# A Mamba-2 scan and ReGLU kernel: pairs 4 and 5 turned by DMA, block 0's tail in another order, its stores issued by GpSimd

## The chip, the core and the metric

The kernel runs on one core of a Trainium2 chip. A core has five engines, each with an instruction queue of its own that it works through in order: TensorE (PE in the profile, its weight loads PEld), VectorE (DVE), ScalarE (ACT), GpSimd (POOL) and SyncE (SP), which here does nothing but issue DMA transfers. They meet through semaphores. The metric is the device time of one execution in microseconds (us); the kernel before takes 122.76 us, the median of three runs from 122.37 to 123.28.

## The reference

Four batches of eight heads with 768 steps each go through a state-space scan in chunks. Its output, 3072 tokens by 256 features, goes through a gated feed-forward layer. Cut to what matters:

```python
for c in range(nc):                                  # chunks of the sequence
    cum = np.cumsum(log_a[:, :, sl], axis=-1)
    L = np.exp(cum[:, :, :, None] - cum[:, :, None, :]) * causal
    y[:, :, sl] = ((Cc @ Bc.T) * L) @ xc             # inside the chunk
                + (Cc @ state) * np.exp(cum)         # from the chunks before
    state = np.exp(sum(la)) * state + (Bc * decay_from_j).T @ xc
gate = np.maximum(X @ w_gate, 0.0)                   # X: [3072, 256], w: [256, 1536]
out  = (gate * (X @ w_val)) @ w_out                  # w_out: [1536, 256]
```

`B` and `C` have 16 features a head, `x` has 32.

## The kernel before

The kernel uses chunks of 128 steps, two chunks of one batch to a **pair**: there are twelve pairs, three to a batch, and six feed-forward **blocks** of 512 tokens, two pairs each. The decays are not put into the matrix L; they are multiplied into `B` and `C` beforehand (`fac`), so that L becomes a mere causal mask.

A pair goes through these steps. Its raw `B` and `C` (`bcr`) and `x` (`xr`) are loaded by SyncE. They are scaled to bf16 by `scale_bc`, `scale_one` or `scale_padded`; `x` is cast to `xb` by `to_x`. `B` and `C` have to be **turned**, features to the partitions. Up to pair 5 TensorE does that (`transp`, line 389, called by `turn`); `tevac` copies the result out of PSUM, `B` in one copy (`bevac`, BT) and `C` in two (`cevac`, CT), each with half of the heads masked to zero. From pair 6 on (`NDMA = 6`) GpSimd writes the scaled `B` and `C` into a zero-padded tile `bz` (`turned`, three in rotation), and one DMA transpose, issued by SyncE on line 306, gives the turned tile `TT`. For the first four pairs, which are laid out "wide", the turned `B` is also turned back (`back`, `backevac`, tile `bx`).

Then `G` (line 452), or `G_rows` (line 491) from pair 6 on, makes the products of `C` and `B`, four PSUM banks a pair. `gevac` brings them to `gs` under the causal mask: ScalarE copies one and a half banks, which GpSimd masks in place (`causal`, line 171), and VectorE masks the others while it copies (lines 475 and 479). `Dm` (line 630), the visit of D, multiplies `gs` with `x`; `inter` (line 619) adds the part of the state, both into the tile `y`; `yevac` copies `y` to `yT`, the feed-forward's input. `state`, `states` (line 569) and `states_two` (line 693) add the products of `B` and `x` into the state's bank `A_ps`, `spread` and `sums_two` take the running sum to the form that `inter` wants. From block 2 on two pairs are taken together (`Dm_two`, line 678).

A block's feed-forward is, for each of its twelve slices of 128 of the 1536 features, `gv` (gate and val on 512 tokens, line 738) or two `gvh` (256 tokens each, line 753): ScalarE applies the relu (`r`), VectorE multiplies (`h`). `fout` (line 783) multiplies `h` with `w_out`, and `foevac` copies the result `o` to `ob` and stores it.

The order is written out by hand. `in_order` ties every engine to the order of the program's text, so a wait of one instruction holds all that stand behind it on its engine. Block b works on its own feed-forward and, between its matmuls, on pairs P = 2b+2 and Q = 2b+3, which block b+1 needs; W = 2b+1 is the pair that the block before left to be finished. The shared PSUM banks are five (`bank`), and the tags "tp", "y" and "Aps" have one bank each.

SyncE's queue is a list too: loads, DMA transposes and stores are issued in the text's order. GpSimd's list holds the masks, the scaling of later pairs and the casts of their `x`; the loop of block 2 calls `scale(Q + 2)`, that is pair 9, just before the masks of pairs 6 and 7.

Of the kernel before, what the change touches and what calls it, by code (L numbers as in the profile page):

```python
# [8 lines left out]
FP32 = mybir.dt.float32  # L9
# [20 lines left out]
def kernel(  # L30
# [71 lines left out]
    def load(p, q):  # L102
        if "bcr" not in st.setdefault(p, {}):
            new_bc(p)
        load_bc(p, 1, q)
        load_bc(p, 0, q)
        new_x(p)
        for i in range(2):
            load_x(p, i, q)
# [182 lines left out]
    def scale_padded(p, eng):  # L292

        b, c0, _ = place(p)
        z = turned[p % 3]
        f = fac[:, b, c0:c0 + 2].rearrange("s i j h -> s i (j h)")
        eng.tensor_tensor(  # L297
            out=z.rearrange("s (i k) (h n) -> s i (k h) n", k=4, n=N)[:, :, 0:2 * NH],
            in0=st[p]["bcr"].rearrange("s i j h n -> s i (j h) n"),
            in1=f.to_broadcast([128, 2, 2 * NH, N]), op=ALU.mult)  # L300
        parts = z.rearrange("s (i k) (q t n) -> s i k t q n", k=4, q=4, t=2)
        for t in range(2):
            eng.tensor_copy(out=parts[:, :, 2 + t, t], in_=parts[:, :, 1, t])
        st[p]["B"] = [z[:, 4 * i] for i in range(2)]
        tt = st[p]["TT"] = att.tile([128, 8, 128], BF16, tag="TT", name="TT", bufs=4)
        nc.sync.dma_start_transpose(out=tt, in_=z.rearrange("s k n -> s (k n)"))

    def new_bs(p):
        st[p]["bs"] = att.tile([128, 4, 128], BF16, tag="bs", name="bs", bufs=6)
# [59 lines left out]
    def scale(p, eng):  # L369
        if p >= NDMA:  # L370
            scale_padded(p, eng)
        else:
            new_bs(p)
            scale_bc(p, eng)
        to_x(p, eng)
# [41 lines left out]
    def ct(p, i, rows=slice(0, 128), t=None):  # L417
        if p < NWIDE:
            c = st[p]["CT"][rows, :, :, 64 * i:64 * i + 64]
        else:  # L420
            c = st[p]["CT"][rows, :, i]
        return c if t is None else c[:, t]

    def split(p, ap):

        return ap.rearrange("s t (r m) -> s t r m", r=2) if p < NWIDE else ap
# [17 lines left out]
    def G(p):  # L444
        s = st[p]
        if "gp" not in s:
            G_banks(p)
        g = s["gp"]
        for i in range(2):
            for q in range(4):  # L450
                r = slice(32 * q, 32 * q + 32)
                nc.tensor.matmul(  # L452
                    out=split(p, g[q][:, i]), lhsT=s["BT"][r, i], rhs=ct(p, i, r),
                    start=(i == 0), stop=True, tile_position=(32 * q, 0),
                    skip_group_check=True)
        s["gs"] = att.tile([128, 4, 4, 128], BF16, tag="gs", name="gs", bufs=2)
# [70 lines left out]
    def state(p, i):  # L527
        astep(p, i)
        sevac(p, i)
# [93 lines left out]
    def Dm(p, apart=False):  # L623
        s = st[p]
        y_bank(s, apart)
        for t in range(2):
            for i in range(2):
                new = opening(s, t)
                for q in range(4):
# [4 lines left out]
                        start=new, stop=True,  # L634
                        tile_position=(0, 32 * q), skip_group_check=True)

    def yevac(p, *engs):
        s = st.pop(p)
        dst = yT[:, :, p * 256:(p + 1) * 256]
        if p >= NWIDE:  # L640
            copy(engs[0], dst.rearrange("q t (i m) -> q t i m", i=2), s["ya"])
            return
        for t in range(2):
            copy(engs[t % len(engs)],
                 dst[:, t].rearrange("q (i m r) -> q i r m", i=2, r=2),
                 s["y"][t].rearrange("q i (r m) -> q i r m", r=2))
# [154 lines left out]
    def foevac(b, ts, o=None):  # L801
        last = b == NBLK - 1 and ts == 2
        if ts % 2 == 0 and not last:
            return
        ob = ffn.tile([128, 2, DM], FP32, tag="ob", name="ob", bufs=3)
        r0 = b * 512 + ts * 128
        if last:
            nc.scalar.copy(out=ob[:, 0], in_=fst["o"][:, 0])
            nc.scalar.dma_start(out=out[r0:r0 + 128, :], in_=ob[:, 0])
            return  # L810
        nc.scalar.copy(out=ob, in_=o or fst["o"])  # L811
        rows = out[r0 - 128:r0 + 128, :].rearrange("(i p) m -> p i m", p=128)
        for part in ((slice(0, 1), slice(1, 2)) if b in (2, 3) and ts == 3 else (slice(0, 2),)):
            nc.sync.dma_start(out=rows[:, part], in_=ob[:, part])


    B_, C_ = slice(0, 1), slice(1, 2)
# [89 lines left out]
    def turn(p):  # L907
        transp(p, 1)
        transp(p, 0)

    def tevac(p, beng, *cengs):
        bevac(p, beng)
        cevac(p, *cengs)
# [49 lines left out]
    for b in range(NBLK):  # L963
        P, Q, W = 2 * b + 2, 2 * b + 3, 2 * b + 1
        more = P < NPAIR
        if b == 1:
            load(P + 2, nc.sync)
            load(P + 3, nc.sync)
        if b == 2:
            scale(Q, nc.gpsimd)  # L970
            load(Q + 2, nc.sync)

        nh = (4, 6, 8, 0)[min(b, 3)]
        for f in range(nh):
            if b == 0:
                continue
            turning = f == (3 if b == 1 else nh - 3)
            gvh_mm(b, f, 0)
            gvh_relu(b, f, 0)
            gvh_mul(b, f, 0)  # L980
            if b == 1 and f == 1:
                to_x(P, nc.scalar)
            if turning:
                inter(W, 0)
                inter(W, 1)
                Dm(W)
                if b == 1:
                    states(P)
                    scale_one(P, nc.gpsimd, 1)
                else:  # L990
                    states_two((P, Q))
                yevac(W, nc.scalar)
                if b == 1:
                    spread(P)
                else:
                    sums_two((P, Q))
# [4 lines left out]
        for f in range(nh, NF):  # L1001
            gv(b, f, b > 2 and f == 0)
            if b == 0:
                if f == 5:
                    over_sum(de_ps)
                if f == 7:
                    sevac(1, 1)
                if f == 9:
                    turn(P)
                    tevac(P, nc.scalar, nc.vector)  # L1010
                if f == 10:
                    held(Q, bc=False)
                if f == 11:
                    back(P)
                    backevac(P, nc.scalar)
            elif b == 1:
                if f == nh:
                    turn(P)
                    tevac(P, nc.scalar, nc.vector)
                    scale(Q, nc.gpsimd)  # L1020
                if f == 8:
                    turn(Q)
                    tevac(Q, nc.scalar, nc.vector)
                    scale(Q + 1, nc.gpsimd)
                    load(Q + 3, nc.sync)
            elif b == 2:
                if f == 9:
                    scale(Q + 2, nc.gpsimd)
                    load(Q + 3, nc.sync)
                    load(Q + 4, nc.sync)  # L1030
            elif b == 3:
                if f in (2, 6):
                    scale(P + 2 + f // 4, nc.gpsimd)
# [3 lines left out]
        if b == 0:  # L1037

            for third in range(3):
                fs = range(4 * third, 4 * third + 4)  # L1040
                fout(b, 0, fs)
                fout(b, 1, fs)
                if third == 0:
                    new_bc(Q + 1)
                    nc.vector.memset(st[Q + 1]["bcr"][0:1, 0, 0, 0, 0:1], 0.0)
                    load_bc(Q + 1, 0, nc.sync)
                    new_x(Q + 1)
                    for i in range(2):
                        load_x(Q + 1, i, nc.sync)
                    load_bc(Q + 1, 1, nc.sync)  # L1050
                    for n in range(1, NB):
                        nc.vector.reciprocal(fac[:, n, :, 0], fac[:, n, :, 1])
                if third == 0:
                    turn(Q)
                if third == 1:
                    G(P)
                    gevac(P)
                    tevac(Q, nc.scalar, nc.vector)
            foevac(b, 1)
            to_x(Q, nc.scalar)  # L1060
            fout(b, 2)
            state(P, 0)
            state(P, 1)
            held(Q + 2)
            back(Q)
            backevac(Q, nc.vector)
            fout(b, 3, range(6))
            inter(P, 0)
            inter(P, 1)
        elif b == 1:  # L1070
            fout(b, 0)
            G(P)
# [36 lines left out]
            continue  # L1109
        Dm(P)  # L1110
        states(Q)
        if b == 0:
            yevac(P, nc.vector)
            G(Q)
            gevac(Q, after={3: lambda: spread(Q)})
            new_bs(Q + 1)
            scale_one(Q + 1, nc.gpsimd, 0)
        else:
            yevac(P, nc.scalar)
            G(Q)  # L1120
            spread(Q)
            gevac(Q)
        fout(b, 3, range(6, NF) if b == 0 else range(NF))
        foevac(b, 3)

    in_order(tc)
# [30 lines left out]
```

## Time and profile before

| | |
|---|---|
| three runs | 122.37, 122.76, 123.28 us |
| profiled execution | 122.67 us |
| its span, first to last instruction | 121.0 us |
| granted TensorE clock | 1.00 |
| busy: PE, DVE, ACT, POOL | 115.5, 89.0, 74.3, 51.5 us |
| packets of SyncE's loads, transposes and stores | 73088, 10.54 MB |
| DMA transposes | 6, 256 KB of bf16 each |

A line of a timeline gives the start in us from the span's beginning, the length, the engine, the kernel's line, the operation, the tile written and the tile read, and how many instructions are merged; in square brackets stands how long the engine had been idle and what ended that. "SPq" marks the issue of a DMA on SyncE; the length of such a line is that of the issue, not of the transfer. The chain of work that ended last is followed back from the last instruction, at each step to what released it. A full digit row (9) in a slice means 90% or more.

### The profile page before, as it was taken

The page shows a single profiled execution, that of the slowest core. Times are in us where ns is not written, and L with a number is a line of the kernel's source. Part 1 is how long each engine was busy: PE and PEld are TensorE (multiplying, and loading weights), DVE is VectorE, ACT ScalarE, POOL GpSimd, SP SyncE. Part 2 cuts the span into 40 slices and gives each one's busy share as a digit, 9 for nine tenths or more (in the row PEclk, how much of TensorE's full clock was granted, in tenths as well). Part 3 has the DMA queues.
Part 4 walks back from the last instruction along what each step waited for, and adds up shares of the span by engine and source line. Part 5 has one row for each costly group of instructions (what it writes and reads, how often), then busy time and mean ns, then how long its engine had stood idle before and what let it go on. Part 6 is the DMA issues. An engine that isn't in the chain of part 4 may idle for free.

```text
span 121.0 us, 3322 instructions
## 1 busy us (share of the span) xinstructions
PE 115.5 (95%) x1231; PEld 74.8 (62%) x1238; DVE 89.0 (74%) x214; ACT 74.3 (61%) x161; POOL 51.5 (43%) x104
## 2 busy tenths in 40 slices
PE   7789999999999999999999999999999999999990
PEld 2245864577885477888487544578444677444790
DVE  5888888977999956899875687866778675678500
ACT  4166886843998744888734767525767445766340
POOL 6879999831705252857084363433400033000000
PEclk9999999999999999999999999999999999999999
DMA  3999999999989999899978799962200002200022
GB/s 67 208 172 162 201 186 188 207 141 130 161 99 170 125 105 131 106 202 182 115 138 136 80 107 152 197 127 78 95 5 0 0 0 92 87 0 0 0 87 87
DMA packets 80591, 13.69 MB, mean 113 GB/s; under 512 B 73424, under 2 KB 80576, under 8 KB 80576
## 3 DMA queue, kind: packets, MB, share of 16 engines
q1 hardware_dynamic: 73088, 10.54, 56.9%
q0 software_dynamic: 4080, 2.36, 14.0%
q10 hardware_dynamic: 3408, 0.59, 2.6%
q8 instruction: 9, 0.15, 0.5%
q14 instruction: 6, 0.05, 0.1%
HBM read 11.12 MB, written 3.15 MB: 118 GB/s over the span
## 4 chain that ended last, share of the span: by engine, by line
PE 89%; DVE 3%; DMA 3%; issue 1%; SPq 1%; ACT 0%; DVEq 0%
PE o L783 26%; PE gate L738 19%; PE val L738 19%; PE gv L753 13%; DMA bcr<-in_C_dram 3%; PE g L452 2%; PE g L491 2%; PE y L678 1%; PE y L630 1%; PE o L795 1%; DVE bs L344 1%; PE tp L389 1%; DVE gs L475 1%; PE y L619 1%; PE y L665 0%
## 5 line engine op out<-in xcount | busy, mean ns | idle before, releaser
L742 DVE TENSOR_TENSOR h<-r,val 128x512 bf16<-128x512 bf16 x54 | 36.7, 686 | 9.3 <-ACT r L741 6.4
L741 ACT ACTIVATE r<-gate 128x512 bf16<-128x512 f32 x54 | 32.3, 597 | 11.9 <-PE gate L738 10.9
L783 PE MATMUL o<-wo,h 128*128 128x256 bf16 x276 | 33.7, 273 | 0.0
L738 PE MATMUL gate<-yT,wg 128*128 128x512 bf16 x105 | 32.0, 379 | 0.2
L738 PE MATMUL val<-yT,wv 128*128 128x512 bf16 x105 | 31.5, 379 | 0.2
L783 PEld LDWEIGHTS <-h 128*128 128x128 bf16 x276 | 25.7, 98 | 5.6 <-issue 1.4
L171 POOL TENSOR_SCALAR_AFFINE_SELECT gs<-gs 128x512 bf16<-128x512 bf16 (+1 forms) x24 | 12.2, 531 | 25.3 <-ACT gs L464 25.3
L475 DVE TENSOR_TENSOR gs<-g,masks 128x512 bf16<-128x512 f32 x24 | 15.4, 684 | 6.3 <-PE g L491 2.8
L738 PEld LDWEIGHTS <-wv 128*128 128x128 bf16 x108 | 10.6, 98 | 12.5
L738 PEld LDWEIGHTS <-wg 128*128 128x128 bf16 x108 | 10.4, 98 | 11.1
L464 ACT CAST gs<-g 128x512 bf16<-128x512 f32 x12 | 7.0, 587 | 14.6 <-PE g L452 6.2
L763 DVE TENSOR_TENSOR h<-r,gv 128x256 bf16<-128x256 bf16 x36 | 13.9, 416 | 0.9 <-ACT r L760 0.7
L760 ACT ACTIVATE r<-gv 128x256 bf16<-128x256 f32 x36 | 13.7, 389 | 1.2
L753 PE MATMUL gv<-yT,wg 128*128 128x256 bf16 x72 | 13.9, 273 | 0.0
L753 PE MATMUL gv<-yT,wv 128*128 128x256 bf16 x72 | 13.9, 273 | 0.0
L297 POOL TENSOR_TENSOR bz<-bcr,fac 128x512 bf16<-128x512 f32 x6 | 6.3, 1058 | 9.1 <-DMA bcr<-in_B_dram 9.1
L811 ACT COPY ob<-o 128x512 f32<-128x512 f32 x11 | 6.5, 595 | 4.0 <-PE o L783 4.0
L318 ACT CAST yT<-y 128x512 bf16<-128x512 f32 (+1 forms) x9 | 4.6, 531 | 5.4 <-PE y L678 3.4
L753 PEld LDWEIGHTS <-wv 128*128 128x128 bf16 x72 | 7.0, 98 | 0.8
L753 PEld LDWEIGHTS <-wg 128*128 128x128 bf16 x72 | 6.8, 98 | 1.1 <-issue 0.2
L318 POOL CAST xb<-xr 128x512 bf16<-128x512 f32 (+1 forms) x9 | 5.3, 594 | 3.8 <-DMA xr<-in_x_dram 3.7
L318 DVE CAST yT<-y 128x256 bf16<-128x256 f32 (+1 forms) x7 | 3.7, 550 | 4.0 <-PE y L678 2.0
(119 smaller groups left out, 110.7 us busy)
## 6 DMA issues: line engine op xcount, KB each, us to landing
xr<-in_x_dram SPq DMA_DIRECT2D x23, 128.0 KB, 3.3
out_dram<-ob SPq DMA_DIRECT2D x9, 256.0 KB, 2.5
bcr<-in_B_dram SPq DMA_DIRECT2D x16, 64.0 KB, 3.0
bcr<-in_C_dram SPq DMA_DIRECT2D x16, 64.0 KB, 2.9
wg<-in_moe_w_gate_dram POOLq DMA_DIRECT2D x6, 128.0 KB, 4.8
wv<-in_moe_w_val_dram POOLq DMA_DIRECT2D x6, 128.0 KB, 5.0
wo<-in_moe_w_out_dram POOLq DMA_DIRECT2D x3, 256.0 KB, 7.1
out_dram<-ob SPq DMA_DIRECT2D x4, 128.0 KB, 2.4
```

The lines of the kernel that those rows point to most:

```text
L171: nc.gpsimd.affine_select(out=dst, in_=dst, pattern=pattern, compare_op=ALU.is_ge, fill=0.0, base=0, channel_multiplier=-1)
L318: (eng.copy if eng is nc.scalar else eng.tensor_copy)(out=out, in_=in_)
L464: nc.scalar.copy(out=d[:, 0], in_=g[0])
L475: nc.vector.tensor_tensor(out=d[:, q], in0=g[q], in1=m, op=ALU.mult)
L738: nc.tensor.matmul(out=o, lhsT=w_tile(ws, f, k), rhs=yT[:, k, tk], start=(k == 0), stop=(k == 1), skip_group_check=True)
L741: nc.scalar.activation(r, g, AF.Relu)
L742: nc.vector.tensor_tensor(out=fst[b][:, f], in0=r, in1=v, op=ALU.mult)
L753: nc.tensor.matmul(out=gv_[:, j], lhsT=w_tile((wgs, wvs)[j], f, k), rhs=yT[:, k, tk], start=(k == 0 and not (early and j)), stop=(k == 1), ...
L760: nc.scalar.activation(r[:, 0:256], fst[b, f, u][:, 0], AF.Relu)
L763: nc.vector.tensor_tensor(out=fst[b][:, f, u * 256:(u + 1) * 256], in0=fst.pop((b, f, u, "r"))[:, 0:256], in1=fst.pop((b, f, u))[:, 1], op ...
L783: nc.tensor.matmul(out=o[:, ts % 2], lhsT=fst[b][:, f, ts * 128:(ts + 1) * 128], rhs=wo[:, f], start=(f == 0 and new), stop=(f == NF - 1), ...
L811: nc.scalar.copy(out=ob, in_=o or fst["o"])
```

## The change

Four things are changed.

- **Pairs 4 and 5 are turned by DMA.** A new function `scale_turned` lets GpSimd write their scaled `B` and `C` into the padded tile in four products; `turn_padded`, cut out of `scale_padded`, issues the transpose. `G` and `ct` read `TT` for them. Their `turn`, `tevac`, `scale_one` and `scale` go. Pair 4's are called at the end of block 0, pair 5's at the beginning of block 1, between the loads of pair 6.
- **GpSimd issues block 0's two stores**, not SyncE.
- **Pair 3's turned tiles are copied by ScalarE alone**, right after the transposes, and turned back before `fout(b, 2)`.
- **Block 0's tail is put in another order.** Pair 2's last state product goes into a bank of its own, next to `Dm`; `states(Q)` and `G(Q)` follow before `inter(P)`, and the two halves of pair 2's `y` are copied in the midst of pair 3's `gevac`, one by ScalarE and one by VectorE.

```diff
+    def scale_turned(p, eng):
+        b, c0, _ = place(p)
+        z = turned[p % 3]
+        dst = z.rearrange("s (i k) (q t n) -> s i k t q n", k=4, q=4, t=2)
+        src = st[p]["bcr"].rearrange("s i j (t q) n -> s i j t q n", t=2)
+        f = fac[:, b, c0:c0 + 2]
+        for j in range(2):
+            for t in range(2):
+                eng.tensor_tensor(
+                    out=dst[:, :, j * (2 + t), t], in0=src[:, :, j, t],
+                    in1=f[:, :, j, 4 * t:4 * t + 4].to_broadcast([128, 2, 4, N]), op=ALU.mult)
+        st[p]["B"] = [z[:, 4 * i] for i in range(2)]
+
+    def turn_padded(p):
         tt = st[p]["TT"] = att.tile([128, 8, 128], BF16, tag="TT", name="TT", bufs=4)
-        nc.sync.dma_start_transpose(out=tt, in_=z.rearrange("s k n -> s (k n)"))
+        nc.sync.dma_start_transpose(out=tt, in_=turned[p % 3].rearrange("s k n -> s (k n)"))
...
+    def yevac_half(p, t, eng):
+        dst = yT[:, :, p * 256:(p + 1) * 256]
+        copy(eng, dst[:, t].rearrange("q (i m r) -> q i r m", i=2, r=2),
+             st[p]["y"][t].rearrange("q i (r m) -> q i r m", r=2))
...
-            nc.sync.dma_start(out=rows[:, part], in_=ob[:, part])
+            (nc.sync if b else nc.gpsimd).dma_start(out=rows[:, part], in_=ob[:, part])
...
         if b == 1:
-            load(P + 2, nc.sync)
+            new_bc(P + 2)
+            load_bc(P + 2, 1, nc.sync)
+            load_bc(P + 2, 0, nc.sync)
+            scale_turned(Q, nc.gpsimd)
+            turn_padded(Q)
+            new_x(P + 2)
+            for i in range(2):
+                load_x(P + 2, i, nc.sync)
             load(P + 3, nc.sync)
+            to_x(Q, nc.gpsimd)
...
                     states(P)
-                    scale_one(P, nc.gpsimd, 1)
...
             elif b == 1:
-                if f == nh:
-                    turn(P)
-                    tevac(P, nc.scalar, nc.vector)
-                    scale(Q, nc.gpsimd)
                 if f == 8:
-                    turn(Q)
-                    tevac(Q, nc.scalar, nc.vector)
                     scale(Q + 1, nc.gpsimd)
...
                 if third == 0:
                     turn(Q)
+                    tevac(Q, nc.scalar, nc.scalar)
                 if third == 1:
                     G(P)
                     gevac(P)
-                    tevac(Q, nc.scalar, nc.vector)
+            back(Q)
+            backevac(Q, nc.scalar)
             foevac(b, 1)
             to_x(Q, nc.scalar)
             fout(b, 2)
+            rest = A_ps[0]
+            A_ps[0] = mm.tile([128, 2, 128], FP32, tag="tp", name="A_5")
             state(P, 0)
-            state(P, 1)
-            held(Q + 2)
-            back(Q)
-            backevac(Q, nc.vector)
-            fout(b, 3, range(6))
+            A_ps[0] = rest
+            Dm(P)
+            states(Q)
+            G(Q)
+            held(Q + 2, with_x=False)
+            fout(b, 3, range(3))
             inter(P, 0)
             inter(P, 1)
+            gevac(Q, between=lambda: yevac_half(P, 0, nc.scalar),
+                  after={2: lambda: yevac_half(P, 1, nc.vector), 3: lambda: spread(Q)})
+            scale_turned(Q + 1, nc.gpsimd)
+            turn_padded(Q + 1)
+            new_x(Q + 2)
+            for i in range(2):
+                load_x(Q + 2, i, nc.sync)
+            fout(b, 3, range(3, NF))
+            foevac(b, 3)
+            continue
```

More of the change, by code (lines that the diff above doesn't have):

```diff
@@ L304, in scale_padded @@
         st[p]["B"] = [z[:, 4 * i] for i in range(2)]
+        turn_padded(p)
+    def scale_turned(p, eng):
[11 more added lines that the diff above has]
+    def turn_padded(p):
         tt = st[p]["TT"] = att.tile([128, 8, 128], BF16, tag="TT", name="TT", bufs=4)
-        nc.sync.dma_start_transpose(out=tt, in_=z.rearrange("s k n -> s (k n)"))
+        nc.sync.dma_start_transpose(out=tt, in_=turned[p % 3].rearrange("s k n -> s (k n)"))
     def new_bs(p):
@@ L420, in ct @@
         else:
-            c = st[p]["CT"][rows, :, i]
+            c = st[p]["TT"][rows, 4 * i + 2:4 * i + 4]
         return c if t is None else c[:, t]
@@ L452, in G @@
                 nc.tensor.matmul(
-                    out=split(p, g[q][:, i]), lhsT=s["BT"][r, i], rhs=ct(p, i, r),
+                    out=split(p, g[q][:, i]), rhs=ct(p, i, r),
+                    lhsT=s["BT"][r, i] if p < NWIDE else s["TT"][r, 4 * i],
                     start=(i == 0), stop=True, tile_position=(32 * q, 0),
@@ L1111 @@
         states(Q)
[L1112 to L1123, printed above, removed]
+        yevac(P, nc.scalar)
+        G(Q)
+        spread(Q)
+        gevac(Q)
+        fout(b, 3)
         foevac(b, 3)
```

## The prediction

> **What bounds the kernel now.** I read the engines' shares first, then the chain of work that ended last, then the timelines of the engines that feed it. On the page:
>
> ```profile
> PE 115.5 (95%) x1231; PEld 74.8 (62%) x1238; DVE 89.0 (74%) x214; ACT 74.3 (61%) x161; POOL 51.5 (43%) x104
> DMA  3999999999989999899978799962200002200022
> PE 89%; DVE 3%; DMA 3%; issue 1%; SPq 1%; ACT 0%; DVEq 0%
> ```
>
> TensorE is busy for 95% of the span and holds 89% of the chain; its granted clock is full in every slice. But the DMA row is full too, up to slice 24, about 75 us. The chain in order of time shows which PE pieces the change takes:
>
> ```profile
> 37.81 0.22 PE tp L389 x4
> 39.76 0.22 PE tp L389 x4
> 47.16 0.34 PE y L630 x16
> 66.39 0.56 PE y L678 x32
> ```
>
> The first two are the transposes of pairs 4 and 5 in block 1, with no gap to the gate and val matmuls around them. The last two are the visits of D for pair 4 (`Dm`) and for pairs 6 and 7 (`Dm_two`), which need GpSimd's masks in `gs`. Third, SyncE's own timeline, which issues nearly every load (start, length, instruction, count):
>
> ```profile
> 43.89 1.20 SPq L100 DMA_DIRECT2D xr<-in_x_dram  x2
> 45.19 1.46 SPq L306 DMA_TRANSPOSE TT<-bz  x1
> 46.71 2.12 SPq L92 DMA_DIRECT2D bcr<-in_C_dram  x2
> 48.87 1.54 SPq L92 DMA_DIRECT2D bcr<-in_B_dram  x2
> ...
> 53.20 1.30 SPq L306 DMA_TRANSPOSE TT<-bz  x1
> 54.56 2.28 SPq L92 DMA_DIRECT2D bcr<-in_C_dram  x2
> 56.88 1.37 SPq L92 DMA_DIRECT2D bcr<-in_B_dram  x2
> 58.29 1.50 SPq L100 DMA_DIRECT2D xr<-in_x_dram  x2
> ```
>
> Each piece starts where the one before it ended: the queue runs without a pause from 24.9 to 61.5 us, so whatever is put into it moves everything behind it. Fourth, GpSimd, which turns those loads into TensorE's operands:
>
> ```profile
> 43.27 0.61 POOL L318 CAST xb<-xr 128x512 bf16<-128x512 f32 x1
> 45.18 1.00 POOL L171 TENSOR_SCALAR_AFFINE_SELECT gs<-gs 128x512 bf16<-128x512 bf16 x2 [1.29 <-ACT gs L464]
> ...
> 60.72 1.06 POOL L297 TENSOR_TENSOR bz<-bcr,fac 128x512 bf16<-128x512 f32 x1 [3.86 <-DMA bcr<-in_B_dram]
> 61.84 0.53 POOL L303 COPY bz<-bz 128x128 bf16<-128x128 bf16 x2
> 62.38 0.61 POOL L318 CAST xb<-xr 128x512 bf16<-128x512 f32 x1
> 62.95 1.01 POOL L171 TENSOR_SCALAR_AFFINE_SELECT gs<-gs 128x512 bf16<-128x512 bf16 x2
> 64.96 1.00 POOL L171 TENSOR_SCALAR_AFFINE_SELECT gs<-gs 128x512 bf16<-128x512 bf16 x2 [1.00 <-ACT gs L464]
> ```
>
> At 60.72 it has idled 3.86 us for pair 9's B: a later load is a later GpSimd, one for one. And the masks of pairs 6 and 7, for the PE piece at 66.39, stand behind pair 9's scaling and cast in its order. So the bound is TensorE, with the load queue close behind it, through GpSimd.
>
> **PE.** Removed: 8 transposes, 0.22 + 0.22 = 0.44 us, on the chain. Block 0's end is reordered, with the same instructions. From the A_ps product at 28.16 to the first gv at 30.91 it takes 2.75 us; the same pieces at their undisturbed pitch (A_ps 0.14, bt 0.11, twelve o at 0.109, inter 0.22, D 0.34, the 12 state products 0.09, G 0.33) make 2.54. At most 0.2 is to be won there, and I take it: in the new order each operand is ready before its use (pair 2's sum, on VectorE for 0.22 + 0.42, runs beside D, the state products and G; pair 3's cast on ScalarE, 0.61, beside the 12 matmuls of fout). Best case for PE: -0.64.
>
> **ScalarE and VectorE.** VectorE loses six CT products (0.30 each) and one bx copy (0.28). ScalarE loses two BT copies (0.37) and gains two CT (0.474 in the one row that ScalarE has of it) and one bx (0.39). The new CT sit in the 1.97 us that ScalarE waits before pair 2's g at 25.95; neither engine ends a chain piece in block 1. Zero, with 0.3 either way if the CT overrun that gap.
>
> **GpSimd.** Pairs 4 and 5: eight products at 0.405 instead of four at 0.405 and two at 0.622, +0.4 us. Two stores are issued here: the weight DMAs of this queue took 0.77 each, so 1.5 us. The first is queued behind pair 2's masks and ahead of pair 3's; it needs ScalarE's copy of o, which also precedes pair 3's g in ScalarE's order, and GpSimd idles 3.24 us there. The second stands behind pair 4's products and ahead of pair 5's, wanted only at 47. Zero; the cost without that cover is up to 0.8.
>
> **The new transposes in time.** Pair 4's wait for its products, done about 33.4 (before, its four products ran 31.89 to 33.38), holding SyncE for up to 0.8 us; the six transposes of the trace landed 2.7 to 5.1 us after issue, so about 37 to 39. They are wanted at 42.6. Pair 5's, behind pair 6's B and C, land near 44 to 46, wanted at 47. Both are covered.
>
> **The load queue: the term that decides.** Two stores leave it: 29.90 to 30.83 and 36.14 to 36.77, 1.56 us. Two transposes enter it. One costs, by the fence above, 48.87 - 45.19 = 3.68 us less a C pair of 1.4 (others: 1.18, 1.47, 1.64), so 2.3; the other, 56.88 - 53.20, again 3.68, so 2.3. Bounds: 1.3 if only its own issue counts (rows 1.23 to 1.54); 2.6 with the slowest landing (5.1 against about 2.9 for a load, plus part of the issue). I take 2.3, the two rows that stand in this same stream. Delay of the queue by pair 9: 2 x 2.3 - 1.56 = 3.0 us. Lower end 2 x 1.3 - 1.56 = 1.0; upper end 5.2 if the stores use up as much of the DMA engines from the other queue, 6.0 with the 0.8 of SyncE's wait.
>
> The Trainium skill speaks to that upper end: DMA: Bandwidth & Descriptors, under "Issuing engines are not separate DMA queues", says that transfers run on the same 16 engines whoever starts them, so that moving an issue saves only sequencer time. By it the delay would be some 4.6 rather than 3.0. The issue rows alone cannot decide this.
>
> What 3.0 does, with PE at -0.64:
> - Pair 6's cast ended 43.88, now 46.9. Pair 4's masks follow, 1.0: 47.9. `Dm(4)` would come at 47.16 - 0.64 = 46.5. It waits 1.4; the kernel is then at +0.74.
> - Pair 9's cast ended 62.99, now 66.0. Four masks follow, 2.0: 68.0. `Dm_two` wants the last about 0.1 after its start, which was 66.5 with 0.06 for the semaphore: latest end of the cast 64.4. That is a margin of 1.4 against the old schedule, so the total becomes 3.0 - 1.4 = +1.6, whatever was lost before it.
> - Block 3: pair 11's cast ended 76.9, masks were wanted from 80.04; 3.0 late is hidden. What PE has lost it does not get back, being dense afterwards.
>
> Sum: 122.67 (the profiled execution: span 121.0 and 1.67 around it, 0.09 under the median) + 1.6 = **124.3**. In general, the change is the larger of -0.64 and (delay - 1.4).
>
> **Rivals.**
> 1. *The transposes are nearly free in the queue.* For it: the last two, issued at 59.92 and 62.40, cost little beyond their own 1.5 and 1.2. With 1.0 of delay: 122.67 - 0.4 = 122.3. If one took no longer than the stores it replaces, the delay is nil: 122.67 - 0.64 = 122.0. It is not slower up to a delay of 1.4. Against it: the two 3.68 stretches. The Trainium skill, Advanced Engine Details and Errata, "X-Bar Transpose (TRN2)", says that such transposes are as fast as regular DMAs; by it this rival holds, and it would give the 122.0. The landings of up to 5.1 us here against 2.9 for loads speak against it. Chance 0.25.
> 2. *The DMA engines are the limit, not the issue.* Delay 4.6: +3.2, 125.9. For it: the DMA row of nines. Against it: the row slackens around 36 us. Chance 0.17.
> 3. *A new wait in block 0*, pair 2's halves of y leaving between pair 3's masks: the first gv needs both, and each waits about 0.4 more. On its own, with free transposes, -0.64 + 0.8: 122.8; beside a late queue it is hidden. Chance 0.08.
>
> Forecast: 0.50. A measurement of this kernel can tell about 1% from no change, 1.23 us around 122.76. Of the forecast's half, delays of 1.9 to 4.0 (123.2 to 125.3), some 0.38 lie over 123.99; with rival 2 that is 0.55 slower; 0.40 within (rivals 1 and 3, the rest); 0.05 faster, for a gain in PE that I do not see. Range, from rival 1's end to rival 2's: 122.0 to 125.9.
>
> **What the new profile would show.** Right: no transposes in block 1; two new ones on SyncE with slow loads behind them; GpSimd waiting longer for pair 9's B than before, its cast of pair 9 ending near 66; idle TensorE ahead of `Dm(4)` and `Dm_two`, released by GpSimd's masks. Wrong: that cast ending before 64, and these two visits of D unmoved or earlier; then rival 1 or 3 holds.

## The result

| | before | after |
|---|---|---|
| median of 16 runs, us | 122.78 | 124.31 |
| lowest and highest | 122.37 to 123.37 | 122.81 to 128.25 |
| ratio, 95% interval | | 1.0093 (1.0070 to 1.0117) |
| profiled execution, us | 122.67 | 124.30 |
| its span | 121.0 | 122.6 |

The changed kernel is slower, by 0.9% by the ratio, which leaves out its five slowest runs (124.74 and more) although four of them had the full granted clock (1.00) and only the slowest a lower one (0.983), and by 1.2% by the medians of all runs; the two lie on both sides of the 1% that separated "within" from "slower" in the forecast. The runs spread much more than before.

The page after, in the lines that answer to those shown of before: engines' shares, the DMA row, the chain's shares.

```profile
PE 116.5 (95%) x1223; PEld 74.9 (61%) x1230; DVE 88.0 (72%) x206; ACT 75.3 (61%) x163; POOL 53.4 (44%) x108
DMA  3999999979999997999896879970400002200022
PE 63%; DMA 11%; POOL 10%; SPq 6%; DVE 4%; issue 2%; ACT 1%; POOLq 0%; ACTq 0%
```

TensorE's share of the chain has fallen from 89% to 63%; loads, GpSimd and SyncE's issues hold 27%. SyncE's timeline after:

```profile
33.45 2.75 SPq L323 DMA_TRANSPOSE TT<-bz  x1
36.31 1.14 SPq L100 DMA_DIRECT2D xr<-in_x_dram  x2
37.50 1.48 SPq L92 DMA_DIRECT2D bcr<-in_C_dram  x2
39.02 1.35 SPq L92 DMA_DIRECT2D bcr<-in_B_dram  x2
40.47 1.31 SPq L323 DMA_TRANSPOSE TT<-bz  x1
41.82 1.20 SPq L100 DMA_DIRECT2D xr<-in_x_dram  x2
...
61.41 1.29 SPq L100 DMA_DIRECT2D xr<-in_x_dram  x2
```

The two transposes at 33.45 and 40.47 are the new ones. Behind them, pair 6's x is issued at 41.82 instead of 39.38, 2.4 us late, and pair 9's x at 61.41 instead of 58.29, 3.1 us late. The rows of the kernel before for the first load of pair 6 and for its x:

```profile
36.77 1.18 SPq L92 DMA_DIRECT2D bcr<-in_C_dram  x2
...
39.38 1.38 SPq L100 DMA_DIRECT2D xr<-in_x_dram  x2
```

GpSimd's timeline passes that on:

```profile
45.45 0.61 POOL L335 CAST xb<-xr 128x512 bf16<-128x512 f32 x1 [1.06 <-DMA xr<-in_x_dram]
46.02 1.01 POOL L171 TENSOR_SCALAR_AFFINE_SELECT gs<-gs 128x512 bf16<-128x512 bf16 x2
...
63.96 1.06 POOL L297 TENSOR_TENSOR bz<-bcr,fac 128x512 bf16<-128x512 f32 x1 [4.66 <-DMA bcr<-in_B_dram]
65.08 0.53 POOL L303 COPY bz<-bz 128x128 bf16<-128x128 bf16 x2
65.55 0.61 POOL L335 CAST xb<-xr 128x512 bf16<-128x512 f32 x1
66.12 1.97 POOL L171 TENSOR_SCALAR_AFFINE_SELECT gs<-gs 128x512 bf16<-128x512 bf16 x4
```

Before, the masks of pairs 6 and 7 came in two groups of two, the second after a wait of 1.00 us for ScalarE. Now four of them run in one piece after pair 9's cast, with no idle time: their inputs were there, and only the cast ahead of them held them. TensorE's timeline shows these idle times and no others between 24 and 112 us (before, it showed none in that stretch):

```profile
46.72 0.71 PE L648 MATMUL y<-gs,xb 128*32 128x128 bf16 x16 [0.21 <-POOL gs L171]
...
66.82 0.60 PE L701 MATMUL y<-gs,xb 128*32 128x128 bf16 x8 [0.50 <-POOL gs L171]
67.78 0.82 PE L701 MATMUL y<-gs,xb 128*32 128x128 bf16 x24 [0.36 <-POOL gs L171]
```

All are visits of D, released by GpSimd's masks. The last matmul of the visit of pairs 6 and 7 begins at 68.38, and before it began at 66.73, 1.65 us earlier; the rest of the kernel keeps that distance (85.41 against 83.76, 102.91 against 101.26 for the next two visits' first matmuls). That is the whole loss of this execution, 124.30 - 122.67 = 1.63.

### The profile page after: what moved, and what is told of

Read it like the earlier page. It is cut to its first block, busy times and chain, and to the rows that moved or that the text cites. A ratio compares the mean times of both kernels' runs of the same rounds, so it can differ in the third digit from the quotient of the medians.

```text
span 122.6 us, 3307 instructions
## 1 busy us (share of the span) xinstructions
PE 116.5 (95%) x1223; PEld 74.9 (61%) x1230; DVE 88.0 (72%) x206; ACT 75.3 (61%) x163; POOL 53.4 (44%) x108
## 4 chain that ended last, share of the span: by engine, by line
PE 63%; DMA 11%; POOL 10%; SPq 6%; DVE 4%; issue 2%; ACT 1%; POOLq 0%; ACTq 0%
PE o L806 17%; PE gate L761 16%; PE val L761 15%; PE gv L776 7%; DMA bcr<-in_B_dram 5%; DMA xr<-in_x_dram 5%; SPq L92 4%; POOL gs L171 3%; SPq L323 2%; POOL bz L297 2%; POOL xb L335 1%; POOL wg L153 1%; DMA a_first<-in_a_dram 1%; PE y L701 1%; POOL wv L153 1%
## 5 line engine op out<-in xcount | busy, mean ns | idle before, releaser
L335 ACT CAST yT<-y 128x256 bf16<-128x256 f32 (+1 forms) x10 | 5.0, 522 | 7.7 <-PE y L701 5.1
```

Of the source, the lines that this page charges most:

```text
L335: (eng.copy if eng is nc.scalar else eng.tensor_copy)(out=out, in_=in_)
```

## The experiments

Theory A: the transposes lengthen SyncE's queue, later loads land later, GpSimd casts later, and its masks, which stand behind the casts, hold TensorE. Rivals: the loss comes from block 0's new order or from the stores; the DMA engines and not the queue set the pace; the loads cost time elsewhere too. The edits are against the changed kernel, except where the kernel before is named.

**Pairs 4 and 5 turned by TensorE again**, the rest of the change kept.

```diff
-            scale_turned(Q + 1, nc.gpsimd)
-            turn_padded(Q + 1)
+            new_bs(Q + 1)
+            scale_one(Q + 1, nc.gpsimd, 0)
...
+                if f == nh:
+                    turn(P)
+                    tevac(P, nc.scalar, nc.vector)
+                    scale(Q, nc.gpsimd)
                 if f == 8:
+                    turn(Q)
+                    tevac(Q, nc.scalar, nc.vector)
```

> The changed kernel with pairs 4 and 5 turned by TensorE again (no new transposes by DMA); block 0's new order and GpSimd's stores stay. Theory A (the two transposes delay the loads): no idle TensorE ahead of the visits of D, TensorE has its 0.44 us of transposes back, 122.7, as before; pair 9's cast ends at 62.9 or up to 1.5 us earlier. Rival: if part of the loss lies in block 0's order or in the stores on GpSimd, it stays: 123.5 or more.

Measured: 122.81, ratio 1.0002 (0.9979 to 1.0026). GpSimd's cast and masks, and SyncE's issue of pair 9's x:

```profile
62.70 0.61 POOL L335 CAST xb<-xr 128x512 bf16<-128x512 f32 x1
63.27 1.01 POOL L171 TENSOR_SCALAR_AFFINE_SELECT gs<-gs 128x512 bf16<-128x512 bf16 x2
64.52 1.00 POOL L171 TENSOR_SCALAR_AFFINE_SELECT gs<-gs 128x512 bf16<-128x512 bf16 x2 [0.24 <-ACT gs L482]
```

```profile
58.56 1.50 SPq L100 DMA_DIRECT2D xr<-in_x_dram  x2
```

The masks are two groups again, and the whole loss is gone with the two transposes: neither block 0's order nor the stores on GpSimd cost anything by themselves that shows. But pair 9's x is issued at 58.56, no earlier than the 58.29 of before, although the two stores are not in the queue. The next experiment takes that by itself.

**The kernel before, with block 0's stores on GpSimd.**

```diff
-            nc.sync.dma_start(out=rows[:, part], in_=ob[:, part])
+            (nc.sync if b else nc.gpsimd).dma_start(out=rows[:, part], in_=ob[:, part])
```

> The kernel before with block 0's two stores issued by GpSimd, nothing else. Theory A: SyncE's queue is 1.56 us shorter, GpSimd's cast of pair 9 ends up to 1.5 earlier (or waits longer for a load of the same landing time if the engines are the limit), and since nothing waited for it, the time stays: 122.7. Rival (the stores on GpSimd cost something themselves, through the masks that stand behind them): 123.2 or more.

Measured: 123.00, ratio 1.0011 (0.9985 to 1.0036). No change in time, as expected; and pair 9's x is issued at 58.63, no earlier. At pair 6's C the queue is 0.8 us ahead (35.97 against 36.77), at pair 7's x nothing of it is left (43.95 against 43.89).

```profile
35.97 1.77 SPq L92 DMA_DIRECT2D bcr<-in_C_dram  x2
...
43.95 1.35 SPq L100 DMA_DIRECT2D xr<-in_x_dram  x2
...
58.63 1.52 SPq L100 DMA_DIRECT2D xr<-in_x_dram  x2
```

So the -1.56 of the prediction was not there in this kernel.

**Transposes alone**: the kernel before, with two, then with one more transpose in the queue, into tiles that nobody reads. The first two kernels only add transfers; the third also issues block 0's stores on GpSimd.

```diff
+    def spare(n):
+        t = att.tile([128, 8, 128], BF16, tag="spare", name="spare", bufs=2)
+        nc.sync.dma_start_transpose(out=t, in_=turned[n].rearrange("s k n -> s (k n)"))
...
         if b == 1:
+            spare(1)
             load(P + 2, nc.sync)
+            spare(2)
             load(P + 3, nc.sync)
```

> The kernel before, with two transposes by DMA more in SyncE's queue (one ahead of pair 6's loads, one ahead of pair 7's) of tiles that nobody reads: only work is added. Theory A: delay by pair 9 of 2 x 2.3 = 4.6 us (4.2 by the two of the changed kernel), less the 1.4 of margin: +2.8 to +3.2, 125.5 to 125.9. With transposes that cost only their own issue, 2 x 1.3: +1.2, 123.9. Rival (the loss comes from how the changed kernel waits for its new tiles, not from the queue): 122.8.

> The kernel before with one spare transpose by DMA in SyncE's queue, ahead of pair 6's loads. Two such cost 1.4 us by the ratio of that run. If the loads have a margin of 1.4 us before GpSimd's masks come late, and a transpose costs the queue about 1.4: nothing or 0.2, 122.7 to 122.9. If there is no margin and each one costs its share: half of 1.4, 123.4.

> The kernel before with the two spare transposes and with block 0's stores issued by GpSimd. If taking the stores off SyncE's queue shortens the delay by their 1.56 us of issue: 124.6 less up to 1.5, so 123.1. If their bytes cost the loads as much from the other queue: 124.6, as with the stores on SyncE. By the changed kernel (124.3 with 0.44 us less of TensorE's work) the second is the nearer.

| kernel | median | ratio, interval | its profiled execution: time | pair 9's cast ends | later than before | visit of pairs 8 and 9 begins | later than before |
|---|---|---|---|---|---|---|---|
| before | 122.78 | | 122.67 | 62.99 | | 83.76 | |
| one spare | 123.62 | 1.0094 (1.0058 to 1.0131) | 123.95 | 65.36 | 2.37 | 84.60 | 0.84 |
| two spare | 124.63 | 1.0115 (1.0078 to 1.0151) | 123.35 | 64.77 | 1.78 | 84.01 | 0.25 |
| two spare, stores on GpSimd | 124.41 | 1.0102 (1.0067 to 1.0136) | 124.88 | 66.72 | 3.73 | 85.97 | 2.21 |
| the change | 124.31 | 1.0093 (1.0070 to 1.0117) | 124.30 | 66.16 | 3.17 | 85.41 | 1.65 |

Transfers that nobody waits for, and no other change, make the kernel before slower by 0.9 to 1.15%: a loss of this size needs no wait for the new tiles. (The one padded tile that the single spare transpose reads is next written at 49.86, long after the 3.0 us that the transfer took to land.) Here are the spare kernel's transpose and its effects, with one spare (SyncE, GpSimd, TensorE):

```profile
37.13 1.40 SPq L310 DMA_TRANSPOSE spare<-bz  x1
...
60.66 1.43 SPq L100 DMA_DIRECT2D xr<-in_x_dram  x2
```

```profile
64.74 0.62 POOL L322 CAST xb<-xr 128x512 bf16<-128x512 f32 x1
65.31 1.97 POOL L171 TENSOR_SCALAR_AFFINE_SELECT gs<-gs 128x512 bf16<-128x512 bf16 x4
```

```profile
66.97 0.82 PE L682 MATMUL y<-gs,xb 128*32 128x128 bf16 x24 [0.17 <-POOL gs L171]
```

Pair 9's x is issued 2.4 us later than before (60.66 against 58.29), and the cast ends as much later. Of that, 0.36 was there ahead of the spare transpose, which stands at 37.13 where the kernel before issues its next load at 36.77. So in this execution the transpose, with an issue of 1.40, has moved pair 9's x by 2.0. The expectation that one would stay inside the margin was wrong because it put the price at 1.4.

The margin can be read in each row of the table: how much later the cast ends, less how much later TensorE begins the visit of pairs 8 and 9. It is 1.53, 1.53, 1.52 and 1.52, so a late cast costs TensorE all of its lateness beyond 1.5 us. The rest of the difference in time, 0.44 and 0.43 us in the first two executions with spare transposes, lies behind the last matmul (3.26 and 3.24 us to the end of the span, against 2.83 before); its cause is not shown.

The second spare added little. Two of them were expected to cost 2.8 to 3.2 us by the old price and cost about 1.4 by the ratio. In their execution the queue was 0.65 early at the first spare (36.12 against 36.77) and 1.43 late at pair 9's x: both together moved it by 2.1. With the stores on GpSimd, the same reckoning against the kernel before with those stores (0.78 late at the first spare, 3.38 at pair 9's x) gives 2.6. The runs do not give a price per transpose. The taking away of the stores, 1.0115 against 1.0102, bought nothing that can be told.

**The changed kernel with the stores back on SyncE**, twice.

```diff
-            (nc.sync if b else nc.gpsimd).dma_start(out=rows[:, part], in_=ob[:, part])
+            nc.sync.dma_start(out=rows[:, part], in_=ob[:, part])
```

> The changed kernel with block 0's two stores back on SyncE's queue, all else as changed. Theory A, the loads are late because SyncE's queue is long and its issues are what counts: 1.56 us more delay by pair 9, GpSimd's cast of pair 9 ends at 66.2 + 1.6 = 67.8, and the time is 124.3 + 1.5 = 125.8. Theory B, the 16 DMA engines are what counts, whoever issues: the same bytes and packets, no change against the changed kernel, 124.3.

> The changed kernel with block 0's stores on SyncE, once more and in more rounds, since the run before (125.64, few samples) and the run of the stores alone on the kernel before (no gain for the loads) seem to disagree. If a store's place on SyncE's queue costs its issue in this kernel: 125.5 or more again. If the DMA engines set the pace whoever issues: 124.3.

Measured: 125.64 and 125.47, ratios 1.0214 (1.0166 to 1.0261) and 1.0215 (1.0167 to 1.0263). Beside 1.0093 that is 1.2% more, 1.5 us, as expected if a store costs its issue: in the changed kernel the stores' place does seem to count, where in the kernel before, with or without spare transposes, it did not. The changed kernel itself was not run again beside these two. The second execution, with SyncE's rows of the changed kernel (first fence) and of this one (second fence) and TensorE's idle times:

```profile
25.86 1.16 SPq L92 DMA_DIRECT2D bcr<-in_B_dram  x2
```

```profile
26.44 1.15 SPq L92 DMA_DIRECT2D bcr<-in_B_dram  x2
...
62.00 1.57 SPq L100 DMA_DIRECT2D xr<-in_x_dram  x2
```

```profile
25.77 0.40 PE L406 MATMUL tp<-ident,bs 128*128 128x128 bf16 x4 [1.24 <-POOL bs L361]
48.43 0.71 PE L648 MATMUL y<-gs,xb 128*32 128x128 bf16 x16 [0.27 <-POOL gs L171]
68.50 0.82 PE L701 MATMUL y<-gs,xb 128*32 128x128 bf16 x24 [0.25 <-POOL gs L171]
```

SyncE is 0.58 us later than in the changed kernel at 26.44, ahead of block 0's first store (30.96), 1.45 later at pair 6's x, and 0.59 later at pair 9's: what was added in between is gone again where it would decide. TensorE's wait of 1.24 also stands ahead of the first store, so the store cannot be its cause; one execution of another kernel has it too (the first of those with everything late put off, below), with 1.36. It does not add to the total here, since the visit of pairs 6 and 7 waits for the late masks in any case: the visit of pairs 8 and 9 begins 0.72 later than in the changed kernel, as much as pair 9's cast ends later (66.88 against 66.16), and another 0.43 lies behind the last matmul. So this execution shows no loss that can be put down to the stores. Why the runs with the stores on SyncE are 1.5 us longer stays open.

**GpSimd's masks first.** The loads stay late; what is taken away is what queues behind them: pair 6's cast goes behind pair 4's masks, pair 9's scaling and cast behind the masks of pairs 6 and 7, the state products of pairs 8 and 9 move into block 3.

```diff
                 if f == 8:
-                    scale(Q + 1, nc.gpsimd)
+                    scale_padded(Q + 1, nc.gpsimd)
...
             gevac(P)
+            to_x(Q + 1, nc.gpsimd)
             over_sum2(de)
...
                 if f == 9:
-                    scale(Q + 2, nc.gpsimd)
                     load(Q + 3, nc.sync)
                     load(Q + 4, nc.sync)
             elif b == 3:
+                if f == 1:
+                    states_two((P, Q))
+                    sums_two((P, Q))
...
             gevac(Q)
+            if b == 2:
+                scale(Q + 2, nc.gpsimd)
             foevac(b, 1, first_two)
```

> The changed kernel, with GpSimd's order changed: the masks of pair 4 ahead of the cast of pair 6, the masks of pairs 6 and 7 ahead of pair 9's scaling and cast; the state products of pairs 8 and 9 move into block 3, and pair 9's transpose behind the loads of pairs 10 and 11. The transposes and the late loads stay. Theory A (the late loads cost time only because masks are queued behind them on GpSimd): no idle TensorE ahead of the two visits of D, 122.7 - 0.44 = 122.2, better than both kernels. Rival (the late loads or the queue cost time elsewhere too): 124 or more.

Measured: 122.65, ratio 0.9998 (0.9972 to 1.0023). Pair 9's x is issued at 62.15, later than in the changed kernel, and costs nothing at the visit of D:

```profile
45.35 1.01 POOL L171 TENSOR_SCALAR_AFFINE_SELECT gs<-gs 128x512 bf16<-128x512 bf16 x2
46.55 0.61 POOL L335 CAST xb<-xr 128x512 bf16<-128x512 f32 x1 [0.20 <-DMA xr<-in_x_dram]
...
63.03 1.01 POOL L171 TENSOR_SCALAR_AFFINE_SELECT gs<-gs 128x512 bf16<-128x512 bf16 x2 [3.13 <-ACT gs L482]
65.39 1.00 POOL L171 TENSOR_SCALAR_AFFINE_SELECT gs<-gs 128x512 bf16<-128x512 bf16 x2 [1.36 <-ACT gs L482]
66.37 1.06 POOL L297 TENSOR_TENSOR bz<-bcr,fac 128x512 bf16<-128x512 f32 x1
```

The masks of pairs 6 and 7 wait for ScalarE again and for no load, those of pair 4 stand ahead of pair 6's cast, and TensorE shows no idle time ahead of either visit. That is the proof of the last link. The gain of 0.44 that was expected beyond that does not show in the time. In the profiled execution, the slowest of the ten (123.40), the late loads found a third place, pair 7's cast ahead of the state products of pairs 6 and 7:

```profile
52.76 0.24 PE L716 MATMUL A_ps<-xb,bz 128*32 128x64 bf16 x8 [0.79 <-POOL xb L335]
```

**Only the later place mended** (pair 6's cast left ahead of pair 4's masks).

> The changed kernel with only the later of the two places mended: masks of pairs 6 and 7 ahead of pair 9's scaling and cast, the state products of pairs 8 and 9 in block 3. Pair 6's cast still stands ahead of pair 4's masks. Theory A: the wait ahead of the visit of D of pair 4 stays (0.2 in the changed kernel's profile, up to 1.4), the later one goes: 122.4 to 123.2. Rival (the second place was no cause): 124.3.

Measured: 123.33, ratio 1.0039 (1.0011 to 1.0066): a little over half the way back. The wait that is left ahead of pair 4's visit of D, and another one, in block 0, for the cast of pair 3's x on ScalarE, which itself waited 0.40 for its load:

```profile
29.07 0.27 PE L587 MATMUL A_ps<-xb,bx 128*32 128x64 bf16 x12 [0.29 <-ACT xb L335]
47.37 0.71 PE L648 MATMUL y<-gs,xb 128*32 128x128 bf16 x16 [0.29 <-POOL gs L171]
```

**Pair 4 turned by TensorE, pair 5 by DMA.**

```diff
-            scale_turned(Q + 1, nc.gpsimd)
-            turn_padded(Q + 1)
+            new_bs(Q + 1)
+            scale_one(Q + 1, nc.gpsimd, 0)
+            scale_one(Q + 1, nc.gpsimd, 1)
...
+                if f == nh:
+                    turn(P)
+                    tevac(P, nc.scalar, nc.vector)
```

> The changed kernel with pair 4 turned by TensorE again and only pair 5 by DMA, all else as changed. Theory A: one transpose in, two stores out of SyncE's queue, a delay of 2.3 - 1.6 = 0.7 us or less, inside the 1.4 of margin; TensorE saves four transposes, 0.22. So 122.5, no idle TensorE ahead of the visits of D. Rival (any transposed pair costs its share of the loss, or the loss is in the block that both share): half of the loss stays, 123.5.

Measured: 123.34, ratio 1.0026 (0.9989 to 1.0062), runs from 122.12 to 124.23. It lies between the expectations and does not decide between them. The profiled execution, the slowest of the ten (124.23), has pair 9's x at 61.38 and idle TensorE at the visit of pairs 6 and 7; but its queue was 1.4 us late well before the one transpose (pair 5's x at 34.95 against 33.52 in the kernel before), so it does not show what that transpose does alone.

**Everything late put off.** On top of the masks first, the state products of pairs 6 and 7 behind block 2's half slices and block 1's stores on GpSimd; then, besides, pair 3's state products behind pair 2's `inter`.

```diff
         if b == 2:
+            states_two((P, Q))
+            sums_two((P, Q))
             scale(P + 2, nc.gpsimd)
...
             Dm(P)
-            states(Q)
             G(Q)
...
             inter(P, 1)
+            states(Q)
```

> The kernel with the masks first at both places, and the third use of late loads put off too: the state products of pairs 6 and 7 move behind block 2's half slices; block 1's two stores go to GpSimd as well (1.04 us less on SyncE). Theory A: no wait for late loads is left, TensorE keeps its saving of 0.44: 122.2, better than the kernel before. Rival (new waits in the moved products, or GpSimd's stores ahead of pair 7's scaling): 122.7 or more.

> The kernel with the masks first and all products of late loads put off, and in block 0 pair 3's state products moved behind pair 2's inter, so that they wait no more for the cast of pair 3's x (TensorE idled 0.3 and 0.7 us there in two profiles). Theory: this wait and those for late loads are gone, TensorE keeps its 0.44: 122.3. Rival (the 0.44 is lost elsewhere): 122.7, as the version without this move.

Measured: 122.73, ratio 1.0005 (0.9968 to 1.0042), and 122.84, ratio 1.0012 (0.9989 to 1.0035). No version beats the kernel before. In the second one's execution TensorE shows no idle time between 24 and 118 us. Reckoned from the transposes of pair 2 (21.51 before, 21.32 here, in the chain) its visits of D begin 0.56 us earlier than before for pair 4, 0.35 for pairs 6 and 7, and 0.04 for pairs 8 and 9: the 0.44 was won in block 1 and given back in blocks 2 and 3, where the state products were moved to. In their new places they take 0.23 and 0.20 in the chain, in the old ones 0.12 and 0.09; that is 0.22 of the 0.52 lost. The rest was not traced.

```profile
56.17 0.23 PE A_ps L716 x16
...
68.77 0.20 PE A_ps L716 x12
```

## Why the prediction was right, and where it was not

- **The total**: 124.3 forecast; 124.31 measured as the median, 124.30 in the profiled execution. The sign, the mechanism and the place hold: the transposes out, 1.0002; the transposes alone, slower; the masks first, 0.9998. That the number fits to 0.01 is luck: the runs lie apart by more than 3 us, and by the runs on the kernel before two terms of the sum were off in opposite directions.
- **The delay of the queue**, 3.0 forecast: 3.1 at pair 9's x (58.29 to 61.41). By the runs on the kernel before, its two terms are mis-sized, and the errors nearly cancel. "Two stores leave it ... 1.56 us" came out at nothing there (58.63 against 58.29 with them gone, ratio 1.0011; 1.0115 against 1.0102 beside spare transposes). The step that failed is that an issue's length was taken for its price: SyncE was 0.8 us ahead at pair 6's C, and by pair 7's x the next issues had spent that. "One costs 2.3" roughly fits one spare transpose, 2.0; two cost 2.1 and 2.6, so 2 x 2.3 was too high. But with the stores back the changed kernel did lose 1.5 us, which is what the 1.56 says and what this reading does not explain; which of the two holds in the changed kernel is open.
- **The Trainium skill's rules**, in that light. DMA: Bandwidth & Descriptors, "Issuing engines are not separate DMA queues", says that another issuer saves only sequencer time: the kernel before agrees (ratio 1.0011); the times of the changed kernel seem not to (1.0215 against 1.0093), for a cause that was not found. Advanced Engine Details and Errata, "X-Bar Transpose (TRN2)", has such transposes as fast as regular DMAs: by the time to landing the trace agrees, with a median of 3.3 us for the changed kernel's eight transposes and 3.1 for its loads of x. The prediction had set the slowest transpose, 5.1, against a median of loads, 2.9. What an added regular transfer of 256 KB would do to the loads behind it was not run, so the 2.0 us of a spare transpose does not decide against the Trainium skill.
- **Pair 4's visit of D**, predicted to wait 1.4 us: it lost 0.5. Without a wait it would have begun at 47.09 - 0.44 - 0.17 (the changed execution runs 0.17 earlier at pair 2's transposes) = 46.5; its first matmul was ready at 46.72 and its last began at 47.22, against 46.67 with none. The step that failed: the full 3.0 was put on pair 6's cast, which ended at 46.06, 2.2 late and not 3.0. The delay had not yet grown to its full size.
- **Pairs 6 and 7's visit**: cast predicted to end at 66.0, measured 66.16; the masks at 68.0, measured 68.09; the visit held until then. The margin is the step that carried the forecast: 1.4 forecast, 1.5 in this execution and in the three with spare transposes.
- **TensorE's saving**: 0.44 in block 1 was there. The 0.2 in block 0 was not: from pair 3's transposes to the first gv it took 6.48 us, before 6.47. The step that failed is "each operand is ready before its use": pair 3's state products waited for ScalarE's cast of x. Where the cast was in time, with pairs 4 and 5 back on TensorE (24.25 to 30.50) and with the masks first (24.61 to 30.86), that stretch took 6.25, so the 0.2 can be had, with the new transposes too.
- **Rivals**: "nearly free" is out by the spare transposes; a new wait in block 0 exists, but is the cast's and not the halves' of y, 0.2 us here and 0.3 with only the later place mended. "The engines are the limit", with 125.9, named a cause that is half borne out, at too high a price. The range stopped at that rival's delay of 4.6, although the working's own upper end, 6.0, would have made 127.3. The chances were split between slower (0.55) and within 1% (0.40); the ratio, 1.0093, sits on that line.

## What to carry to other kernels

An in-order engine that takes in loads is a way by which DMA time turns into TensorE time: before anything is put into a full DMA queue, follow the last load behind it to the engine that waits for it, and ask what stands behind that wait; the slack there is the whole budget, here 1.5 us. The length of a DMA's issue is not its price in a full queue, neither for one put in nor for one taken out; a spare transfer that nobody reads measures it, if one reckons from where the queue stood just ahead of it and takes more than one execution. Order on the consuming engine can hide such a delay entirely, without touching the queue.

## What was not expected of the hardware

- One spare transpose of 256 KB, issued in 1.40 us, moved loads that came 23 us later by 2.0 us; the second added far less (2.1 for both; ratios 1.0094 and 1.0115).
- Issues of about 2.0 to 3.4 us recur near the same times whichever transfer stands there: near 34 us it was the x of pair 5 in the kernel before (2.52) and the transpose of pair 4 in the changed one (2.75). Part of the price read off the old transposes may have been these.
- The changed kernel spreads: 122.81 to 126.31 in 15 of its 16 runs, where the kernel before kept to 122.37 to 123.37. That this comes from its hanging on the load queue is not shown; single runs of the kernel before, beside other experiments, reached 125.33.
